# Pairing half-height matmuls as row tiles of TensorE in a matrix-LSTM followed by a rational feed-forward

## The chip, the cores and the metric

The kernel runs on one core of a Trainium2 chip (trn2). The metric is the device time of one execution in microseconds (us), of which the median of three runs is taken. A core has five engines that run side by side, each in the order of its own instruction stream: TensorE (PE, with its weight loads as PEld), VectorE (DVE), ScalarE (ACT), GpSimd (POOL) and SyncE (SP), which here issues nearly all DMAs. TensorE writes to PSUM, eight banks of 128 partitions by 512 f32 values.

## The reference

A matrix LSTM runs over 768 time steps for 4 batches and 8 heads of width 40, and its output, as 3072 tokens of 320 features, goes through a feed-forward layer whose activation is a rational function. Inputs are drawn at random; the feed-forward weights arrive as 64-bit floats.

```python
for t in range(S):
    m_new = np.maximum(f_gate[:, :, t] + m, i_gate[:, :, t])
    f_stab = np.exp(f_gate[:, :, t] + m - m_new)
    i_stab = np.exp(i_gate[:, :, t] - m_new)
    C = f_stab[..., None, None] * C + i_stab[..., None, None] * np.einsum('bhd,bhe->bhde', vt, kt)
    n = f_stab[..., None] * n + i_stab[..., None] * kt
    h_tilde = np.einsum('bhde,bhe->bhd', C, qt)
    denom = np.maximum(np.abs(np.einsum('bhd,bhd->bh', n, qt)[..., None]), 1.0)
    y[:, :, t] = sigmoid(o_gate[:, :, t]) * h_tilde / denom
...
h = x @ w_in                        # 320 -> 2048
P = a[0] + a[1] * h + a[2] * h**2 + a[3] * h**3
Q = 1.0 + np.abs(b[0]) * np.abs(h) + np.abs(b[1]) * h**2
out = (P / (Q + 1e-06)) @ w_out     # 2048 -> 320
```

## The kernel before

Time is cut into chunks of 64. One **unit** (`attention(u)`, 24 of them) is one batch over 128 time steps, that is two chunks, for all 8 heads. In a unit TensorE transposes keys and queries (`kq`), multiplies them to scores (`f_S`, tiles `ps0`, `ps1`: 16 matmuls of 40 rows by 64 columns that sit on the four 64x64 quadrants of the array), and VectorE multiplies the scores by the decay (`f_P`). Then `f_ow` sums each chunk's contribution to the state, for each head one matmul with all 128 rows and 64 columns of the array and 82 moving columns, whose value tile `vb` is half zeros, into a bank of its own, `ow`. VectorE adds that to the decayed state (`update`, in the list `u0` and `u1`), GpSimd decays the state (`d0`, `d1`). Two units make a **pair** (`outputs(m)`, 12 of them): `f_it` (16 matmuls of 128x64) and `inter` (32 or 16 on quadrants) write the read-out `y`, ScalarE takes the absolute normalizers (`f_ab`) into an SBUF tile `na`, VectorE inverts them (`f_rc`), and the result is transposed into tokens (`f_xt`, tile `px`) and split into a rounded part and a rest (`f_xh`, `f_xl`) in the tile `xk`.

A pair's 256 tokens are one **block** of the feed-forward. `feed_forward(n, i)` is step i (0 to 7) of block n: it handles two chunks of 128 hidden features. The 320 input features are three slices of 128, 128 and 64, each as rounded part and rest, so that a chunk takes eight matmuls of 256 columns into the bank `h` (in the trace `ph`): six with `wi`, one with `wj`, which has the 64-row slice of rounded weights twice, against rounded tokens above and their rest below, and one with `wY`, which has the rest of the 64-row slice of the weights in its upper 64 rows and zeros below:

```python
parts = [
    (w[:, 0, 0], 0), (w[:, 1, 0], 0), (w[:, 0, 1], 1), (w[:, 1, 1], 1),
    (w[:, 0, 0], 2), (w[:, 0, 1], 3), (wX, 4), (wY[:, c * P : (c + 1) * P], 4),
]
```

The activation then goes over ScalarE (`ha`, `p1`, `u`, `y`, `r0`), VectorE (`p3`, `gh`, `m`, `gl`) and GpSimd (`w`, `rm`), and `f_f2` multiplies the result, again as rounded part `gH` and rest `gL`, by `wo` into two banks `po`: per step 16 matmuls of 320 columns with `gH`, 8 with `gL`. All other PSUM tiles share six banks, the ring `h`; a tile takes a bank at its first write and gives it back with its last read.

Each step of work is an entry of a plan (`plan.add` with what it reads and writes). The text `ORDER` lists all entries in the order in which they are issued, so it fixes the stream of every engine; `_Ordered` keeps it. An entry is named by its step: `f1_5_2` is the first matmul of block 5, step 2, and `.1` marks the second of that name. At the start TensorE also runs 90 dummy matmuls (`hot`), and the weights are brought from 64 bits to rounded part and rest by ScalarE, VectorE and GpSimd.

Of the kernel before, what the change touches and what calls it, by code (L numbers as in the profile page):

```python
# [12 lines left out]
I32 = mybir.dt.int32  # L13
# [144 lines left out]
hot.63 hot.64 hot.65 hot.66 gate.11 raw_j0 o2_o0 ogl_0 o2_o3 qa_1 o0_i1 hot.67 P_1 P_1.1 s1_i3 gate.3 s0_i6 s1_i6
s3_i6 ow_1 o2_i1 s0_j1 s2_j1 s3_i3 o0_i3 hot.68 hot.69 hot.70 hot.71 hot.72 o2_i3 lk_2 s1_j1 hot.73 s3_j1 u0_1 o0_i6
o2_i6 s0_i2 gate.18 ogl_2 d1_1 pf_2 it_0 it_0.1 i1_0 sc_2 gate.12 o0_j1 o2_j1 lq_2 hot.74 lk_3 hot.75 s2_j0 s2_i2  # L160
s0_j0 ab_0 hot.76 s1_i2 s3_i2 hot.77 kp_2 o2_j1.1 ke_2 s1_j0 ogl_1 s3_j0 ogl_3 tk_2 ek_2 squares gate.19 ab_0.1 raw_o7
hot.78 hot.79 hot.80 hot.81 o0_j0 lq_3 gate.21 gate.13 hot.82 u1_1 gate.14 raw_i7 tq_2 eq_2 pf_3 kp_3 S_2 P_2 P_2.1
o2_j0 oc_j0 raw_o2 og_0 tk_3 ek_3 o2_j0.1 s0_o7.1 sc_3 gate.15 rc_0 s2_o7 hot.83 g_0 x_0 g_0.1 hot.84 hot.85 hot.86
lf_4 o0_i2 tq_3 s0_o7 s1_o7.1 ke_3 hot.87 hot.88 s3_o7.1 eq_3 x_0.1 xt_0 hot.89 gate.16 lv_2 s1_o7 s3_o7 gate.1 xh_0
xh_0.1 o0_o7 lk_4 s0_i7 S_3 oc_j1 xl_0 s2_i7 xl_0.1 f1_0_0 f1_0_0.1 gate.17 lv_3 P_3 s1_i7 qa_2 s0_o2.1 s1_o2.1 s0_o2
s2_o2 qa_3 raw_i5 o2_o7 o2_i2 f1_0_1 s3_o2.1 ow_2 ha_0_0 u_0_0 gate.20 lk_5 f1_0_1.1 s1_o2 P_3.1 u0_2 f1_0_2 s3_o2
w_0_0 d1_2 p1_0_0 p3_0_0 s3_i7 y_0_0 kp_4 o0_o2 o2_o2 sc_4 r0_0_0 u1_2 ow_3 gh_0_0 ha_0_1 u0_3 la_4 u_0_1 p1_0_1 lq_4
d1_3 m_0_0 f1_0_2.1 ha_0_2 p1_0_2 u1_3 p3_0_1 it_1 it_1.1 i1_1 w_0_1 rm_0_0 p3_0_2 ab_1 ab_1.1 rc_1 gl_0_0 u_0_2 y_0_1
tk_4 g_1 x_1 s0_i5 s2_i5 s1_i5 s3_i5 ke_4 w_0_2 f2_0_0 f2_0_0.1 f3_0_0 g_1.1 la_5 r0_0_1 y_0_2 r0_0_2 ek_4 kp_5 lq_5
f1_0_3 f1_0_3.1 f1_0_4 f3_0_0.1 ha_0_3 u_0_3 tq_4 eq_4 gh_0_1 m_0_1 f2_0_1 x_1.1 gh_0_2 p1_0_3 m_0_2 d0_4 o0_i7  # L170
f1_0_4.1 ha_0_4 rm_0_1 gl_0_1 o0_i5 p3_0_3 w_0_3 y_0_3 raw_o6 S_4 f2_0_1.1 f3_0_1 P_4 f3_0_1.1 f2_0_2 tk_5 f2_0_2.1
rm_0_2 gl_0_2 P_4.1 p1_0_4 r0_0_3 gh_0_3 ek_5 p3_0_4 o2_i5 m_0_3 f1_0_5 f3_0_2 f3_0_2.1 tq_5 f2_0_3 f1_0_5.1 f2_0_3.1
f1_0_6 u_0_4 qa_4 w_0_4 raw_o4 s0_o4.1 s1_o4.1 lf_5 lf_6 s2_o4 s3_o4.1 rm_0_3 eq_5 s0_o6.1 s0_o4 s2_o6 sc_5 lk_6 s1_o4
s1_o6.1 s3_o4 gl_0_3 y_0_4 r0_0_4 f1_0_6.1 gh_0_4 lv_4 o0_o4 ha_0_5 f3_0_3 ke_5 ogl_10 lv_5 lq_6 s3_o6.1 S_5 p1_0_5
ogl_6 f3_0_3.1 m_0_4 P_5 o2_i7 f1_0_7 f1_0_7.1 s0_o6 ha_0_6 u_0_5 o2_o4 s1_o6 P_5.1 rm_0_4 f2_0_4 s3_o6 u_0_6 p1_0_6
xt_1 gl_0_4 f2_0_4.1 ow_4 f3_0_4 p3_0_5 f3_0_4.1 xh_1 xh_1.1 xl_1 xl_1.1 o0_o6 u0_4 kp_6 tk_6 p3_0_6 w_0_5 y_0_5
r0_0_5 w_0_6 y_0_6 d1_4 u1_4 gh_0_5 m_0_5 la_6 f1_1_0 f1_1_0.1 r0_0_6 ek_6 qa_5 gh_0_6 d0_5 ow_5 gate.24 rm_0_5 u0_5
m_0_6 f2_0_5 ha_0_7 ha_1_0 u_0_7 p1_0_7 f1_1_1 f1_1_1.1 f2_0_5.1 gl_0_5 d1_5 gate.22 u1_5 u_1_0 p3_0_7 f3_0_5 f3_0_5.1
gate.23 lk_7 lf_7 lq_7 ogl_7 ogl_8 w_0_7 y_0_7 it_2 it_2.1 i1_2 ogl_11 rm_0_6 gl_0_6 tq_6 r0_0_7 gh_0_7 m_0_7 o2_o6
f2_0_6 f2_0_6.1 ha_1_1 p1_1_0 p1_1_1 p3_1_0 lv_6 sc_6 w_1_0 lv_7 p3_1_1 eq_6 rm_0_7 f3_0_6 f3_0_6.1 u_1_1 ab_2 y_1_0  # L180
w_1_1 r0_1_0 ab_2.1 gh_1_0 gl_0_7 f1_1_2 f1_1_2.1 ha_1_2 y_1_1 r0_1_1 rc_2 g_2 f2_0_7 f2_0_7.1 m_1_0 x_2 f3_0_7
# [190 lines left out]
def _program(  # L372
# [327 lines left out]
    def setup():  # L700
# [729 lines left out]
```

## Time and profile before

| | us |
|---|---|
| median of 3 runs | 514.77 (514.66 to 520.2) |
| profiled execution | 514.69 |
| its span, first to last instruction | 512.9 |
| TensorE busy in the span | 483.8 |
| VectorE, GpSimd, ScalarE busy | 426.0, 404.9, 402.4 |

The span is what the trace covers; some 1.8 us of the execution lie around it. Nearly every instruction is recorded under line 34, the helper that keeps the order, so instructions are told apart by the tile that they write and the tiles that they read (`ph<-xk,wY`) and by their shape. A shape such as 128*64 128x82 is rows times columns of the array that are in use, then the operand. A matmul on plain f32 tiles (`ps`, `ow`, `y`) shows as two records, one on fp32r tiles (`ph`, `po`) as one. The time of one matmul in the trace runs until its result has left the array, so it is longer than the distance at which matmuls follow one another; what a matmul costs is read from the distance between starts.

### The profile page before, as it was taken

What the parts mean: (1) busy time and instruction counts of PE and PEld (TensorE: products, weight loads), DVE (VectorE), ACT (ScalarE), POOL (GpSimd) and SP (SyncE); (2) the same over time, 40 slices, a digit from 0 to 9 for tenths busy, and PEclk for the clock granted to TensorE, in tenths of its full rate; (3) what the DMA queues carried; (4) which work ended last, traced back from release to release, by engine and by line L of the source; (5) the groups of instructions that cost most, each with busy time, mean ns of one, the idle gap of its engine ahead of it and who ended that gap; (6) DMA issues with size and microseconds to landing.
All of it is one profiled execution on the core that took longest, in us unless ns stands there. A gap on an engine that the chain in (4) does not pass through costs nothing.

```text
span 512.9 us, 14161 instructions
## 1 busy us (share of the span) xinstructions
PE 483.8 (94%) x5631; PEld 465.4 (91%) x5631; DVE 426.0 (83%) x702; ACT 402.4 (78%) x698; POOL 404.9 (79%) x375
## 2 busy tenths in 40 slices
PE   6898779999999999999999999999999999999991
PEld 6797679989999999999999999999999999999990
DVE  7889789889898988898797987877878787787890
ACT  1887788978798787788887789898778788869960
POOL 3679778989899988878787898868777889776770
PEclk9899899999999999999999999999999999999996
DMA  6998897415244341532422335311240120000001
GB/s 169 213 273 161 192 255 123 72 27 123 54 99 104 92 77 25 138 77 70 81 54 58 83 75 102 89 25 49 45 96 19 34 72 0 8 23 1 27 0 33
DMA packets 119117, 42.53 MB, mean 83 GB/s; under 512 B 103554, under 2 KB 111810, under 8 KB 119042
## 3 DMA queue, kind: packets, MB, share of 16 engines
q1 hardware_dynamic: 118912, 41.37, 37.0%
q8 instruction: 46, 0.75, 0.6%
q14 instruction: 29, 0.24, 0.2%
q10 hardware_dynamic: 130, 0.16, 0.1%
HBM read 36.90 MB, written 4.10 MB: 80 GB/s over the span
## 4 chain that ended last, share of the span: by engine, by line
PE 71%; DVE 9%; ACT 5%; DMA 4%; POOL 4%; issue 3%; SPq 1%; POOLq 0%; DVEq 0%; ACTq 0%
PE ph L34 29%; PE po L34 27%; PE y L34 4%; PE kq L34 3%; PE ow L34 3%; PE ps L34 2%; DMA rawo<-in_moe_w_out_dram 2%; DVE p L34 2%; POOL p L34 2%; DVE w L34 1%; PE px L34 1%; DMA rawi<-in_moe_w_in_dram 1%; DVE gL L34 1%; ACT ph L34 1%; DVE gH L34 1%
## 5 line engine op out<-in xcount | busy, mean ns | idle before, releaser
L34 POOL TENSOR_TENSOR p<-p,w 128x512 f32<-128x512 f32 (+1 forms) x97 | 129.5, 1335 | 56.4 <-DVE w L34 55.1
L34 PE MATMUL ph<-xk,wi 128*128 128x256 f32 x1152 | 167.5, 281 | 0.7 <-DVE pm L34 0.4
L34 PEld LDWEIGHTS ph<-xk,wi 128*128 128x128 f32 x1152 | 150.3, 188 | 1.8 <-ACT lo0i L34 0.6
L34 POOL TENSOR_TENSOR w<-w,ha 128x512 f32<-128x512 f32 (+1 forms) x97 | 129.9, 1343 | 10.7 <-ACT w L34 10.2
L34 PE MATMUL po<-wo,gH 128*128 128x320 f32 x768 | 135.5, 312 | 0.1
L34 PEld LDWEIGHTS po<-wo,gH 128*128 128x128 f32 x768 | 115.4, 188 | 1.3 <-DVE gH L34 0.3
L34 DVE SCALAR_TENSOR_TENSOR w<-w,gH 128x512 f32<-128x512 f32 (+1 forms) x97 | 89.5, 922 | 3.9
L34 ACT ACTIVATE ph<-w,cd 128x512 f32<-128x512 f32 (+1 forms) x97 | 66.5, 686 | 28.8 <-POOL w L34 14.4
L34 DVE SCALAR_TENSOR_TENSOR gL<-p,ps,ph 128x512 fp32r<-128x512 f32 (+1 forms) x97 | 71.0, 733 | 21.0 <-POOL p L34 20.0
L34 DVE SCALAR_TENSOR_TENSOR gH<-p,ps,ph 128x512 fp32r<-128x512 f32 (+1 forms) x97 | 71.2, 734 | 15.9 <-ACT ph L34 14.6
L34 PE MATMUL po<-wo,gL 128*128 128x320 f32 x384 | 79.8, 318 | 4.3 <-DVE gL L34 4.2
L34 ACT ACTIVATE w<-ha,ba 128x512 f32<-128x512 f32 (+1 forms) x97 | 78.4, 811 | 3.0
L34 DVE SCALAR_TENSOR_TENSOR p<-p,ps,ph 128x512 f32<-128x512 f32 (+1 forms) x97 | 70.6, 733 | 10.8 <-ACT p L34 10.6
L34 ACT ACTIVATE ha<-ph 128x512 f32<-128x512 f32 (+1 forms) x97 | 57.2, 592 | 24.4 <-PE ph L34 23.6
L34 ACT ACTIVATE p<-ph,ps 128x512 f32<-128x512 f32 (+1 forms) x97 | 65.5, 676 | 2.1 <-DVE gL L34 1.8
L34 PEld LDWEIGHTS po<-wo,gL 128*128 128x128 f32 x384 | 59.0, 188 | 7.5 <-DVE gL L34 6.5
L34 ACT ACTIVATE ph<-ph 128x512 f32<-128x512 f32 (+1 forms) x97 | 56.1, 579 | 2.1
L34 PE MATMUL ph<-xk,wY 128*128 128x256 f32 x192 | 53.5, 279 | 0.0
L34 PE MATMUL ph<-xk,wj 128*128 128x256 f32 x192 | 53.4, 278 | 0.0
L34 PEld LDWEIGHTS ph<-xk,wj 128*128 128x128 f32 x192 | 36.2, 188 | 0.0
L34 PEld LDWEIGHTS ph<-xk,wY 128*128 128x128 f32 x192 | 36.1, 188 | 0.0
L34 POOL TENSOR_TENSOR qA<-qT,ab 104x512 f32<-104x512 f32 x24 | 32.0, 1334 | 0.0
(128 smaller groups left out, 658.7 us busy)
## 6 DMA issues: line engine op xcount, KB each, us to landing
rawo<-in_moe_w_out_dram SPq DMA_DIRECT2D x8, 640.0 KB
ab<-scrA SPq DMA_DIRECT2D x40, 128.0 KB
rawi<-in_moe_w_in_dram SPq DMA_DIRECT2D x8, 512.0 KB
qn<-in_q_dram SPq DMA_DIRECT2D x24, 160.0 KB
kr<-in_k_dram SPq DMA_DIRECT2D x24, 160.0 KB
og<-in_o_gate_dram SPq DMA_DIRECT2D x48, 80.0 KB
vb<-in_v_dram SPq DMA_DIRECT2D x48, 80.0 KB
out_dram<-ot SPq DMA_DIRECT2D x23, 160.0 KB
```

The source lines that it names most:

```text
L34: made = fn(*args, **kwargs)
```

## The change

- **Half matmuls.** `wY` is now half as wide and carries the rest of two steps' weights, one in its upper 64 rows, one in its lower. A new entry `f0` for each two steps i and i+1 opens the banks of both and issues four matmuls of 64 rows by 128 columns, alternating between the upper rows (step i) and the lower rows (step i+1); `f1` is left with seven matmuls a chunk. The tokens' rounded 64-row slice is needed in the lower rows too, so ScalarE copies it a second time (`xh` has three entries a pair, `xk` six slices).
- **Step order.** The two steps of an `f0` must use the two halves of `wY`, so step i handles chunks 2*PI[i] and 2*PI[i]+1, with PI = 0, 4, 1, 5, 2, 6, 3, 7.
- **State sums.** `f_ow` issues 16 matmuls of 64 rows, 64 columns and 41 moving columns on quadrants, chunk 0 into the rear of score bank `ps0`, chunk 1 of `ps1`. The bank `ow` is gone; `ps0` is given back after `u0`, `ps1` after `u1`.
- **Normalizers.** `f_ab` writes both halves to the rear of the bank of `y0`, and `f_rc` reads them there.
- **Weights.** The rest of the 64-row slice is loaded in four pieces instead of two; the clearing of `wY`'s lower half by GpSimd goes.
- **List.** `ORDER` is a new list over the new entries.

```diff
-    wY = wp.tile([P, DFF], F32R, name="wY")
+    wY = wp.tile([P, DFF // 2], F32R, name="wY")
...
-            subtract(wY[0:L, c : c + n], z[rr[j]], t[rr[j], cols[j]])
+            subtract(wY[rr[j], s * n : (s + 1) * n], z[rr[j]], t[rr[j], cols[j]])
...
-            ow = d["ow"] = bank("ow")
-            for h in range(H):
-                p, j = divmod(h, 2)
-                nc.tensor.matmul(
-                    ow[j * L : (j + 1) * L, p * 2 * E1 : (p + 1) * 2 * E1],
-                    d["pm"][:, h, 0:L],
-                    vs[:, h].rearrange("p c e -> p (c e)"),
...
+            d["ow"] = [d["ps"][c][:, NP * L :] for c in range(2)]
+            for p in range(NP):
+                for j in range(2):
+                    for c in range(2):
+                        r = slice(c * L, (c + 1) * L)
+                        nc.tensor.matmul(
+                            d["ow"][c][j * L : (j + 1) * L, p * E1 : (p + 1) * E1],
+                            d["pm"][r, 2 * p + j, 0:L],
+                            vs[r, 2 * p + j, c],
...
-        add("ow", "PE", 0.85, f_ow, r=["pm.1", "pm.00", "pm.01", V], w=["ow"], new=new("ow"))
+        add("ow", "PE", 0.85, f_ow, r=["pm.1", "pm.00", "pm.01", V], w=["ps0", "ps1"])
...
-            nc.scalar.copy(xk[nb][:, 0:2, tk] if x == 0 else xk[nb][0:L, 4, tk], pm(x))
+            nc.scalar.copy((xk[nb][:, 0:2, tk], xk[nb][0:L, 4, tk], xk[nb][L:P, 5, tk])[x], pm(min(x, 1)))
...
+    PI = [c // 2 + c % 2 * NS // 2 for c in range(NS)]
...
+        def f_f0():
+            at = iter(plan.many["h"])
+            for x in range(2):
...
+                    FD[n, i + x]["h", j] = ring(psH, "h", [P, W], f"ph{n}_{i + x}_{j}", at=next(at))
+            for j in range(2):
+                for x in range(2):
+                    t, r = FD[n, i + x], slice(x * L, (x + 1) * L)
...
+                    nc.tensor.matmul(
+                        to[:, 0:T], wY[r, c : c + P], xk[n][r, 4 + x, 0:T], start=own, stop=False, skip_group_check=True
+                    )
...
-                (w[:, 0, 0], 2), (w[:, 0, 1], 3), (wX, 4), (wY[:, c * P : (c + 1) * P], 4),
+                (w[:, 0, 0], 2), (w[:, 0, 1], 3), (wX, 4),
```

**TensorE around the start of a block, before.** `px` are the transposes of new tokens, `ph` the hidden features of step 0 of a block.

```order
L34 MATMUL px_6_4022<-ident,xn_3818 128x128 x4
L34 MATMUL px_6_4023<-ident,xn_3818 64x128 x2
L34 MATMUL ph_0_0_4030<-xk_3546,wi_442 128x256 x6
L34 MATMUL ph_0_0_4030<-xk_3546,wj_776 128x256
L34 MATMUL ph_0_0_4030<-xk_3546,wY 128x256
L34 MATMUL ph_0_0_4030<-xk_3546,wi_442 128x256 x6
L34 MATMUL ph_0_0_4030<-xk_3546,wj_776 128x256
L34 MATMUL ph_0_0_4030<-xk_3546,wY 128x256
L34 MATMUL po_0_3608<-wo_451,gL_5_4000 128x320
```

**The same place after.** The first row is the last of a unit's scores, `ph_0` and `ph_1` are the banks of steps 0 and 1 of the block.

```order
L34 MATMUL ps_12_3497<-qT_127,kT_3262 64x64
L34 MATMUL ph_0_0_3514<-xk_2914,wY 128x256
L34 MATMUL ph_1_0_3515<-xk_2914,wY 128x256
L34 MATMUL ph_0_0_3514<-xk_2914,wY 128x256
L34 MATMUL ph_1_0_3515<-xk_2914,wY 128x256
L34 MATMUL ph_0_0_3514<-xk_2914,wi_359 128x256 x6
L34 MATMUL ph_0_0_3514<-xk_2914,wj_723 128x256
L34 MATMUL ph_0_0_3514<-xk_2914,wi_359 128x256 x6
L34 MATMUL ph_0_0_3514<-xk_2914,wj_723 128x256
L34 MATMUL ph_1_0_3515<-xk_2914,wi_444 128x256 x6
L34 MATMUL ph_1_0_3515<-xk_2914,wj_723 128x256
```

The two `wY` matmuls of each step have left the chunks and stand together ahead of two steps' chunks, and both steps' banks are written from there on; here they follow the scores directly.

**TensorE around a unit's state sums, before.** The two `ow` are two units, between the second product of one step and the first product of another.

```order
L34 MATMUL po_0_3608<-wo_905,gL_7_4172 128x320
L34 MATMUL po_1_3609<-wo_905,gL_7_4172 128x320
L34 MATMUL ow_4179<-vb_62,pm_3857 64x82 x8
L34 MATMUL ow_4205<-vb_129,pm_4099 64x82 x8
L34 MATMUL ph_3_0_4214<-xk_3546,wi_646 128x256 x6
L34 MATMUL ph_3_0_4214<-xk_3546,wj_725 128x256
```

**State sums after.** These rows are the last two of one unit's 16 (`ps_12_...<-vb,pm`), then the next `f0` and the second product of an earlier step.

```order
L34 MATMUL ps_12_3496<-vb_62,pm_3493 64x41
L34 MATMUL ps_12_3497<-vb_62,pm_3493 64x41
L34 MATMUL ph_2_0_3636<-xk_2914,wY 128x256
L34 MATMUL ph_3_0_3637<-xk_2914,wY 128x256
L34 MATMUL ph_2_0_3636<-xk_2914,wY 128x256
L34 MATMUL ph_3_0_3637<-xk_2914,wY 128x256
L34 MATMUL po_0_3108<-wo_1209,gH_7_3561 128x320 x2
L34 MATMUL po_1_3109<-wo_1209,gH_7_3561 128x320 x2
```

A unit's state sums are now 16 matmuls of 41 columns that alternate between the two score banks; in this place an `f0` follows them. Over the whole program the shape of the tile that TensorE works with (128x128, 128x64, 64x64, 64x128; transposes count as 128x128) changes 119 times in the stream before and 207 times in the stream after. Of the 48 `f0`, in 46 stretches, 27 stretches come after 128x128 work and 19 after 64x64 work; 43 are followed by 128x128 work and 3 by 64x64 work.

## Rows read from the trace of the kernel before

**Rows 1.** The page: engines' busy time, and the chain by engine

```profile
PE 483.8 (94%) x5631; PEld 465.4 (91%) x5631; DVE 426.0 (83%) x702; ACT 402.4 (78%) x698; POOL 404.9 (79%) x375
...
PE 71%; DVE 9%; ACT 5%; DMA 4%; POOL 4%; issue 3%; SPq 1%; POOLq 0%; DVEq 0%; ACTq 0%
```

**Rows 2.** Busy time by stretch, us; (x) is instructions; then PEclk, DMA share, GB/s

```profile
0.00:60.00 60.00, 48.95 (x713) 45.34 (x714) 49.18 (x121) 40.18 (x73) 40.51 (x51) 0.94 0.89 208
60.00:110.00 50.00, 45.80 (x563) 42.00 (x562) 44.26 (x75) 42.69 (x77) 43.50 (x40) 1.00 0.68 130
...
200.00:300.00 100.00, 99.95 (x1210) 96.86 (x1206) 85.64 (x131) 81.97 (x140) 82.85 (x76) 1.00 0.37 79
```

**Rows 3.** TensorE's waits: us in total, times, longest us

```profile
PE po L34 <- DVE gL L34: 4.2, 8, 1.1
```

**Rows 4.** Groups by shape: busy us, mean ns of one, idle us before

```profile
L34 PE MATMUL ph<-xk,wY 128*128 128x256 f32 x192 | 53.5, 279 | 0.0
...
L34 PEld LDWEIGHTS ph<-xk,wY 128*128 128x128 f32 x192 | 36.1, 188 | 0.0
...
L34 PEld LDWEIGHTS ow<-vb,pm 128*64 128x64 f32 x384 | 14.9, 136 | 3.7 <-issue 1.5 <-DVE zo L34 0.6 <-DVE gL L34 0.2
...
L34 PEld LDWEIGHTS ps<-qT,kT 40*64 40x64 f32 x768 | 13.6, 135 | 4.1 <-issue 1.1 <-ACT qT L34 0.9 <-ACT wo L34 0.2
...
L34 ACT CAST xk<-px 64x256 fp32r<-64x256 f32 x12 | 4.4, 367 | 0.0
```

**Rows 5.** Timeline of PE, us 256 to 258: start, time to last end

```profile
256.21 0.87 PE L34 MATMUL ph<-xk,wi 128*128 128x256 f32 x6
256.92 0.28 PE L34 MATMUL ph<-xk,wj 128*128 128x256 f32 x1
257.04 0.28 PE L34 MATMUL ph<-xk,wY 128*128 128x256 f32 x1
257.15 0.75 PE L34 MATMUL po<-wo,gL 128*128 128x320 f32 x4
```

**Rows 6.** Timeline of PE, us 286 to 290: the scores between whole-array work

```profile
286.30 0.28 PE L34 MATMUL ph<-xk,wY 128*128 128x256 f32 x1
286.50 0.69 PE L34 MATMUL ps<-qT,kT 40*64 40x64 f32 x32
287.13 0.85 PE L34 MATMUL po<-wo,gL 128*128 128x320 f32 x4
287.81 1.33 PE L34 MATMUL po<-wo,gH 128*128 128x320 f32 x8
288.99 0.75 PE L34 MATMUL po<-wo,gL 128*128 128x320 f32 x4
```

**Rows 7.** Timeline of PE, us 273 to 277: reading out a pair

```profile
273.62 0.28 PE L34 MATMUL ph<-xk,wY 128*128 128x256 f32 x1
273.82 1.35 PE L34 MATMUL y<-vb,pm 128*64 128x82 f32 x32
275.11 0.68 PE L34 MATMUL y<-st,qA 40*64 40x41 f32 x32
275.59 0.66 PE L34 MATMUL y<-sm,qA 40*64 40x41 f32 x32
276.18 0.86 PE L34 MATMUL po<-wo,gH 128*128 128x320 f32 x4
276.88 0.75 PE L34 MATMUL po<-wo,gL 128*128 128x320 f32 x4
```

**Rows 8.** Timeline of PE, us 265 to 268: state sums of two steps

```profile
265.18 0.74 PE L34 MATMUL po<-wo,gL 128*128 128x320 f32 x4
265.86 1.35 PE L34 MATMUL ow<-vb,pm 128*64 128x82 f32 x32
267.14 0.96 PE L34 MATMUL ph<-xk,wi 128*128 128x256 f32 x6
267.94 0.28 PE L34 MATMUL ph<-xk,wj 128*128 128x256 f32 x1
```

More of the change, by code (lines that the diff above doesn't have):

```diff
@@ L804, in loads @@
             for j in range(2):
-                c = (2 * j + s) * n
-                yield raw[rr[j]].rearrange("p f w -> p (f w)"), w_in[2 * P : DM, c : c + n].bitcast(I32)
+                for h in range(2):
+                    c = (2 * j + s) * n + h * n // 2
+                    to = raw[rr[j], h * n // 2 : (h + 1) * n // 2].rearrange("p f w -> p (f w)")
+                    yield to, w_in[2 * P : DM, c : c + n // 2].bitcast(I32)
         def high(t, z):
@@ L983, in update @@
         def update(c, dst):
[L985 removed]
+            own = d["ow"][c][0:DP, 0 : NP * E1].rearrange("p (n e) -> p n e", n=NP)
             if n + c == 0:
@@ L1040, in attention @@
             outputs(u // 2)
-        add("u1", "DVE", 0.66, lambda: update(1, st[now]), r=["t1"], w=["ow", *ST3])
+        add("u1", "DVE", 0.66, lambda: update(1, st[now]), r=["t1"], w=["ps1", *ST3])
     def outputs(m):
@@ L1077, in f_ab @@
         def f_ab(k):
[L1078 to L1080 removed]
+            to = d[0][:, NA + k * H : NA + (k + 1) * H].rearrange("p (h c) -> p h c", h=4)
+            nc.scalar.activation(to, ye(k)[:, :, :, D], AF.Abs)
         def f_rc():
[L1083 removed]
+            d["na"] = ring(ap1, "na", [P, 2, H], f"na{m}")
+            nc.vector.tensor_scalar(
+                d["na"], d[0][:, NA : NA + 2 * H].rearrange("p (k h) -> p k h", k=2), 1.0, None, op0=ALU.max
+            )
             nc.vector.reciprocal(d["na"], d["na"])
@@ L1150, in outputs @@
         first = [(X, ("xk", XB))] if m == firsts_of[nb] else ()
-        for x in range(2):
-            add("xh", "ACT", 0.42, lambda x=x: f_xh(x), r=[px[x]], w=[f"{X}.{m - firsts_of[nb]}{x}"], new=first if x == 0 else ())
+        for x in range(3):
+            add("xh", "ACT", 0.42, lambda x=x: f_xh(x), r=[px[min(x, 1)]], w=[f"{X}.{m - firsts_of[nb]}{x}"], new=first if x == 0 else ())
         for x in range(2):
@@ L1338, in each @@
                 )
-        xs = [f"xk{n}.{j}{x}" for j in range(size) for x in range(2)]
+        xs = [f"xk{n}.{j}{x}" for j in range(size) for x in range(3)]
+        if i % 2 == 0:
+            hs = [f"h{n}_{i}"]
+            hs += [f"h{n}_{i + 1}p{j}" for j in range(2)] if n == len(SIZES) - 1 and i + 1 >= NS - HALVED else [f"h{n}_{i + 1}"]
+            ws = [f"wj{PI[i] // 2}{x}" for x in ("", ".l")]
+            plan.add(
+                f"f0_{n}_{i}", "PE", 0.25, f_f0, [xs[1], xs[2], *ws], [*hs, "turn f0"], [(h, ("h", BANKS)) for h in hs]
+            )
         for j in range(2):
             f = chunk(j)
-            add("f1", "PE", 0.9, lambda j=j: f_f1(j), w=["h"], new=[("h", ("h", BANKS))] if j == 0 or last else (), part=j,
-                r=[*xs, f"wi{f // 2}", f"wi{f // 2}.l",
-                   *(f"wj{f % 8 // 4}{x}" for x in ("", ".x", ".l"))])
+            add("f1", "PE", 0.82, lambda j=j: f_f1(j), w=["h"], part=j,
+                r=[*xs, f"wi{f // 2}", f"wi{f // 2}.l", *(f"wj{f % 8 // 4}{x}" for x in ("", ".x"))])
         each("ha", "ACT", 0.48, f_ha, w=["h", "ha"], tag="ha")
```

369 lines of the change are left out of this document (184 added, 185 removed).

## The prediction

> **What bounds the kernel now.** I read the page's busy times first: TensorE is busy for 94% of the span, VectorE for 83%, the others for less, and the chain that ended last runs over TensorE for 71% [rows 1]. An average hides stages, so the table by stretch comes second. Up to 110 us TensorE is busy for 48.95 + 45.80 = 94.75 us, part of that with dummy matmuls; from 200 to 300 us it is busy for 99.95 of 100, at a granted clock of 1.00, which is the 2.4 GHz level, while VectorE, ScalarE and GpSimd stand at 82 to 86 [rows 2]. Third, the waits of TensorE: the largest entry is 4.2 us in 8 waits for the last vector operation of a step [rows 3]. So from about 110 us on the time is the length of TensorE's own stream, and whatever the change does to the other engines is hidden as long as they stay under it. "Busy" means occupied, not working at its peak. What the stream is made of shows only in the timeline, fourth, by the distance between starts.
>
> **Prices from the timeline.** Six matmuls of 256 columns take 256.92 - 256.21 = 0.71 us, so one takes 0.118, and the `wY` one takes as long (0.11 to the next start) although half of its rows are zeros [rows 5]. Eight `po` matmuls take 1.18 us, 0.148 each [rows 6]. On quadrants 32 records take 275.59 - 275.11 = 0.48 us, 0.015 each [rows 7].
>
> Next to these there is a price that no busy time shows: a change of tile shape. From the start of `wY` at 286.30 to the second `po` group at 287.81 are 1.51 us [rows 6]. One `wY` (0.12), 32 records on quadrants (0.48) and four `po` (0.59) explain 1.19. The other 0.32 are two changes, from 128x128 to 64x64 and back, 0.16 each. One sees it directly too: `ps` starts 0.20 after `wY`, where 0.11 is usual. The two units' sums from 265.18 to 267.94 are 2.76 us; without four `po` (0.59), six `wi` (0.71) and two changes (0.32), 1.14 stay for 32 records of `ow`, 0.57 a unit [rows 8]. The read-out confirms it with three changes: 3.26 us, less 0.12, 0.59, 32 records of 128x64 work (1.14) and 64 on quadrants (0.96), leaves 0.45, which is 0.15 for each, and one of these, from 128x64 to 64x64, changes the rows of the tile alone [rows 7]. I take 0.155.
>
> **The change part by part.** The sums are made on TensorE's stream of the profiled execution, 514.69 us, of which 512.9 are span; the median of the runs is 514.77, so nothing has to be scaled.
>
> Half matmuls, gain: 192 `wY` slots of 0.118, 22.6 us, go [rows 4, 5]. In their place are 48 `f0` of two slots each, if the upper and the lower tile run side by side. Quadrant work shows that tiles overlap (0.015 a record against 0.036 for 128x64) [rows 7, 8]. With 0.12 a slot that is 11.5 us, a gain of 11.1. If they do not overlap, the gain is nothing; these are the two ends, and I take the first, as the nearest row (quadrants) overlaps.
>
> Half matmuls, price: 64x128 is a shape of its own. The stream changes shape 207 times instead of 119. I see no row for a change from 128x128 to 64x128; the nearest is the one that changes rows alone, and it is charged [rows 7]. 88 more changes at 0.155 are 13.6 us. A change also lays the first weight load bare, and a load of 128 columns is recorded with 188 ns, one of 64 columns with 136 and 135, whether it has 128 or 40 rows [rows 4]; 46 entries into 64x128 therefore cost another 0.05 each, 2.4 us. Together 16.0. A lone `f0` between 128x128 work is thus 0.24 + 0.31 + 0.05 = 0.60 us against the 0.47 that it replaces; one beside 64x64 work adds one change only, 0.45, and breaks even. The other end: if a change between 128x128 and 64x128 is free, 137 changes are left that are charged, 18 more than before, 2.8 us.
>
> The Trainium skill, TensorEngine Tiling (Array Packing), Key Properties, says that a change of the tiling mode, and not of the tile, drains the engine. This trace agrees for every pair of shapes in it (0.15 to 0.16 us each); for 64x128 no run here shows it, and by that rule the sum stays as it is. The Trainium skill, TensorE: Matmul & The Clock Gate, Part 3 (Packing small matmuls), counts a group of tiles as one matmul plus some 4 ns a tile, with no charge for coming and going. By that rule `f0` only gains, which is the first rival below; the rows for 64x64 speak against it.
>
> State sums: 32 records on quadrants take 0.48 us where 16 of 128x64 took 0.57 [rows 7, 8]; 24 units gain 2.2 us. Their changes of shape are in the count above. Ends: 0 and, if 41 columns ran faster than the read-out's 41 do, hardly more.
>
> Sum over the stream: -11.1 - 2.2 + 16.0 = +2.7 us. About a ninth of the `f0` and a quarter of the units lie ahead of 110 us, where TensorE has slack; nine tenths of it, +2.4, count.
>
> Banks: `f0` needs the banks of both steps at once, a step earlier than before for the second, and `ps0` and `ps1` stay taken until the state is updated, while the bank `ow` is gone. If a bank comes late, the four `f0` matmuls wait, and behind them all that TensorE has in its stream (both steps' chunks, the products of earlier steps, the scores), and then ScalarE waits for `ph`. The nearest row for such a wait is 4.2 / 8 = 0.5 us [rows 3]. I charge two or three of them, 1 us; the low end is nothing.
>
> Nothing for the rest: the third `xh` is 12 copies of 0.367 us, 4.4 us on ScalarE [rows 4], which has 18 of 100 us to spare [rows 2]; if it were late, one `f0` in four would feel it, 12 times 0.37. The normalizers are as many instructions as before. The cleared half of `wY` saves GpSimd work at the start. Four more DMAs are issued by SP at the start, for the same bytes. The new list: at the first steps the other engines have about the same work ahead of them in both streams, so I give it no sign, and 3 us either way, of the 15 that TensorE is not busy ahead of 110 us [rows 2].
>
> Forecast: 514.7 + 2.4 + 1 = **518 us**, no change that a measurement of this kernel can tell, since that takes about 2%, 10 us.
>
> **Rivals.** (1) Coming to and from 64x128 is free. Then -11.1 - 2.2 + 2.8 = -10.5, nine tenths of it -9.4, and with 1 us of waits 506. For it: no row shows this very change. Against it: the change of rows alone in the read-out is charged [rows 7].
> (2) Slower: the two tiles of an `f0` take turns instead of overlapping. Place: each `f0`; price: 96 more slots of 0.118, 11.3 us, nine tenths of them 10, so 528. It decides from where two thirds of the overlap are lost, as 525 is 7 us above the forecast. For it: no row shows tiles with 128 columns side by side. Against: 64x64 tiles in different rows overlap.
> (3) Slower: banks. If half of some 43 `f0` in the bound part wait 0.5 us, 11 us more than the forecast has without waits: 528. For it: two banks of six at once, and score banks that stay taken. Against: one bank less a unit, and a TensorE stream that is longer leaves the others more time.
> (4) Faster: the new list fills the start better and (1) holds in part: half of the price that (1) drops (6 us) and 5 of the 15 us ahead of 110 give 507, all of it and the 5 give 501.
>
> **How the numbers follow.** Forecast 0.60, (1) 0.17, (2) 0.08, (3) 0.08, (4) 0.07. The forecast's own range is 513 to 524, from the list's 3 us and the waits. The 8-in-10 range reaches to (1) below and (2) and (3) above: 505 to 529. Faster by over 2% (under 504.5): a third of (1) and most of (4), 0.11. Slower by over 2% (over 525): most of (2) and (3) and a little of the forecast, 0.17. Within 2%: 0.72.
>
> **What would show it.** In the timeline after: `wY` starts in pairs within some 10 ns, two pairs 0.12 apart (otherwise (2)); the first `wY` starts about 0.20 after a 256-column matmul and the second `wi` after an `f0` about 0.22 after the first (if 0.12 both times, (1)). TensorE should be busy for over 99 of 100 us from 200 to 300; if it is not and `ph` waits for the last vector operation of a step stand in the list of waits, (3). The forecast is wrong if a lone `f0` takes under 0.45 us from its place, or if the start of the steady stretch moves by more than 5 us.

## The result, and the profile after

The changed kernel takes 521.9 us (median of 16 runs, 517.72 to 523.02); the kernel before takes 514.86 us beside it. By the medians it is slower by 7.0 us. The ratio, which is that of the means of the runs, is 1.0118 (6.1 us), with a 95% interval from 1.0097 to 1.0139: a little over 1%, less than the 2% that the forecast set as its line, and 3.9 us above the 518 forecast. The profiled execution took 520.92 us with a span of 519.1, and is the one read here, against 514.69 and 512.9 of before.

The page of the kernel after: busy times by engine, and the chain that ended last, by engine. They answer to [rows 1].

```profile
PE 487.8 (94%) x6015; PEld 458.8 (88%) x6015; DVE 420.3 (81%) x702; ACT 407.7 (79%) x710; POOL 398.3 (77%) x374
...
PE 81%; DVE 5%; SPq 4%; DMA 3%; ACT 2%; issue 2%; DVEq 0%; ACTq 0%
```

TensorE is the bound even more than before, 81% of the chain against 71, and its busy time rose by 4 us. Weight loads take 459 us for 465, though 384 more of them are recorded, those of the state sums. ScalarE has the twelve added copies. (A step has 8 products of 320 columns with `gH` and 4 with `gL`, 768 and 384 in all, and not the 16 and 8 that the description of the kernel gives; the sums of the prediction do not use these counts.) On the engines nothing looks seven microseconds worse, so the next view is the one by stretch, with the columns of [rows 2].

```profile
0.00:60.00 60.00, 49.45 (x813) 45.04 (x813) 46.98 (x117) 37.88 (x68) 35.57 (x49) 0.94 0.89 205
60.00:110.00 50.00, 43.86 (x538) 40.44 (x537) 43.71 (x76) 44.31 (x82) 42.53 (x38) 0.93 0.61 129
110.00:200.00 90.00, 87.74 (x1081) 82.13 (x1080) 78.12 (x120) 71.56 (x124) 75.86 (x70) 0.98 0.34 71
200.00:300.00 100.00, 100.00 (x1275) 94.77 (x1274) 81.76 (x129) 81.82 (x141) 80.22 (x73) 1.00 0.35 74
```

The reader should see two things. From 200 us on TensorE is busy for 100 of 100 us, as forecast. And from 60 to 200 us something is new in the column of the granted clock: 0.93 and 0.98, where before stands at 1.00 from 60 to 110 [rows 2], and from 110 to 200 too. From 60 to 110 TensorE also does less, 43.86 us of busy time against 45.80. Its waits there, in the view of waits from 60 to 120 us (us in total, times, longest us):

```profile
PE po L34 <- DVE gL L34: 2.3, 1, 2.3
PE ph L34 <- DVE zi L34: 2.1, 1, 2.1
PE po L34 <- DVE gH L34: 2.0, 1, 2.0
PE kq L34 <- issue: 1.9, 1, 1.9
```

Four waits of about 2 us each, 8.3 us in all. Before has nine waits in the same stretch, 5.4 us in all, and none is longer than 1.1; the largest entry there is

```profile
PE po L34 <- DVE gL L34: 3.1, 4, 1.1
```

The price of the pairs is read from the timeline of the kernel after (start, time to the last end, operation):

```profile
227.96 0.83 PE L34 MATMUL po<-wo,gL 128*128 128x320 f32 x4
228.71 0.68 PE L34 MATMUL ps<-vb,pm 64*64 64x41 f32 x32
229.32 0.50 PE L34 MATMUL ph<-xk,wY 64*128 64x256 f32 x4
229.75 1.44 PE L34 MATMUL po<-wo,gH 128*128 128x320 f32 x8
231.03 0.75 PE L34 MATMUL po<-wo,gL 128*128 128x320 f32 x4
...
237.66 1.34 PE L34 MATMUL po<-wo,gH 128*128 128x320 f32 x8
238.84 0.45 PE L34 MATMUL po<-wo,gL 128*128 128x320 f32 x2
239.23 0.50 PE L34 MATMUL ph<-xk,wY 64*128 64x256 f32 x4
239.66 0.97 PE L34 MATMUL ph<-xk,wi 128*128 128x256 f32 x6
240.46 0.28 PE L34 MATMUL ph<-xk,wj 128*128 128x256 f32 x1
...
275.67 0.74 PE L34 MATMUL ph<-xk,wY 64*128 64x256 f32 x8
276.34 0.97 PE L34 MATMUL ph<-xk,wi 128*128 128x256 f32 x6
```

A lone `f0` first: from 237.66 to 240.46 are 2.80 us; ten `po` at 0.148 and six `wi` at 0.118 explain 2.19, so four half matmuls with their way in and out cost 0.61 us, where the four whole ones cost 0.47. That the tiles overlap is seen at 275.67: two `f0` in one stretch last 0.67 us to the next start, one lasts 0.43 at 239.23, so four more records take 0.24, which is 0.12 for a pair of an upper and a lower tile. The single starts in the trace say the same: in the long stretch the pairs start at 275.67, 275.89, 276.01 and 276.13, the two tiles of a pair 3 or 4 ns apart. The 0.22 between the first two pairs is the price of coming in; in a lone `f0` it stands between its only two pairs (239.23 and 239.45). Beside 64x64 work, from 227.96 to 231.03, 3.07 us less twelve `po` (1.77) and 32 quadrant records (0.48) leave 0.81; 0.32 of it the quadrants would have cost alone [rows 6], so this `f0` adds 0.49 and about breaks even.

So the tiles of a pair run side by side, and the way in and out costs about what was forecast. What remains to be found is where the seven microseconds come from.

### The profile page after: what moved, and what is told of

The parts are those of the page before. It is cut to its first block, busy times and chain, and to the rows that moved or that the text cites. A ratio compares the mean times of both kernels' runs of the same rounds, so it can differ in the third digit from the quotient of the medians.

```text
span 519.1 us, 14993 instructions
## 1 busy us (share of the span) xinstructions
PE 487.8 (94%) x6015; PEld 458.8 (88%) x6015; DVE 420.3 (81%) x702; ACT 407.7 (79%) x710; POOL 398.3 (77%) x374
## 4 chain that ended last, share of the span: by engine, by line
PE 81%; DVE 5%; SPq 4%; DMA 3%; ACT 2%; issue 2%; DVEq 0%; ACTq 0%
PE ph L34 34%; PE po L34 32%; PE ps L34 5%; SPq L34 4%; PE y L34 4%; PE kq L34 4%; DMA vb<-in_v_dram 2%; PE px L34 1%; DMA rawo<-in_moe_w_out_dram 1%; ACT ph L34 1%; DVE gH L34 1%; DVE gate_f L34 1%; DVE e L34 1%; DVE gL L34 0%; PE hot L34 0%
## 5 line engine op out<-in xcount | busy, mean ns | idle before, releaser
L34 POOL TENSOR_TENSOR p<-p,w 128x512 f32<-128x512 f32 (+1 forms) x97 | 127.1, 1310 | 60.2 <-DVE w L34 58.4
L34 POOL TENSOR_TENSOR w<-w,ha 128x512 f32<-128x512 f32 (+1 forms) x97 | 126.4, 1307 | 10.9 <-ACT w L34 10.6
L34 DVE SCALAR_TENSOR_TENSOR w<-w,gH 128x512 f32<-128x512 f32 (+1 forms) x97 | 79.9, 824 | 5.6
L34 PEld LDWEIGHTS po<-wo,gL 128*128 128x128 f32 x384 | 60.1, 191 | 5.0 <-DVE gL L34 3.6
L34 POOL TENSOR_TENSOR qA<-qT,ab 104x512 f32<-104x512 f32 x24 | 33.6, 1401 | 3.0 <-ACT qT L34 3.0
L34 PE MATMUL hot<-ident 128*128 128x128 f32 x180 | 27.2, 306 | 4.0 <-DVE flag_out L371 4.0
L34 PEld LDWEIGHTS hot<-ident 128*128 128x128 f32 x180 | 24.8, 217 | 4.5 <-issue 4.0
```

The lines of the kernel that those rows point to most:

```text
L34: made = fn(*args, **kwargs)
```

## Experiments

**The change taken apart.** The change has three parts: the list, the state sums on quadrants, and the pairs. Three theories stood against each other, and the expectations name them so: A, that of the prediction, by which the shape changes of the pairs cost somewhat more than the overlap gains, and the list is neutral; B, the pairs gain about 10 us and the list loses more than that; C, the pairs come out even and the list costs it all. The first experiment keeps the list and the quadrants of after and takes the pairing out, with the same number of instructions:

```
-  to[:, 0:T], wY[r, c : c + P], xk[n][r, 4 + x, 0:T], start=own, ...
+  to[:, 0:T], wY[:, c : c + P], xk[n][:, 4, 0:T], start=own, ...
```

> The changed kernel and its list, but the four matmuls of each f0 use all 128 rows (128x128, the paired weights against the token slice of step i), so no tile shape changes for them and nothing overlaps; the sums they add are not the reference's. The stream has 137 changes of shape instead of 207. Theory A (leaving and entering 64x128 costs more than the overlap gives): 70 changes at 0.155 us and 46 long loads at 0.05 go, 11.1 us of overlap go too; net 2 us faster, up to 4 if a lone f0 is 0.63 us against 0.47: 518 to 520. Rival B (pairing pays its 11 us and the loss is made by the list): 10 us slower, 531. Rival C (pairing is worth nothing either way): 522.

Measured: 518.11 us, ratio 1.0055 (1.0037 to 1.0073). The pairs cost 521.9 - 518.1 = 3.8 us in this list, as A has it; B and C don't fit.

The second takes the quadrants out as well, so that of the change the list stays, with what belongs to it: `f0` as an entry of its own ahead of two steps, now at full height, the step order, the third copy, the loads in four pieces, and the sums in a score bank. This is meant by the list alone below.

```
-  d["ow"] = [d["ps"][c][:, NP * L :] for c in range(2)]   # 16 matmuls of 64x64
+  ow = d["ow"] = d["ps"][1]                               # 8 matmuls of 128x64, as before
```

> The changed kernel's list with the old forms of both matmuls: f0 on all 128 rows as in e1, state sums as 8 matmuls of 128x64 with 82 columns, in the second score bank; the hidden features are not the reference's. 129 changes of shape. TensorE's work is then that of before plus ten changes (1.6 us). Theory A with a list that is no better or worse: 516. Rival (the list costs 3 to 5 us at the start, by more waits and a low clock): 518 to 521. Rival B: 525 or more is not expected by any.

Measured: 520.11 us, ratio 1.0092 (1.0061 to 1.0122). The list alone costs 5.2 us against 514.87 beside it; ten of its shape changes (129 for 119) are 1.6 of that by the prediction's price. From here to the first experiment are the quadrants, which gain 2.0 us. So 5.2 - 2.0 + 3.8 = 7.0 us, where each term is a difference of medians and uncertain by one to two us: the largest part is the one that I gave no sign. The quadrants were also taken out with the pairs kept, by the same edit:

> After with its list and its pairs, but the state sums as before: 8 matmuls of 128x64 tiles in the second score bank in place of 16 on quadrants. 24 units times 0.09 us more per unit is +2.2, 8 shape changes fewer at 0.155 are -1.2: +1 us by my terms, 522.5 to 523.5. Rival: the quadrants gain nothing, 521.5 to 522; or more than the row says, 524 to 525.

Measured: 522.43 us, ratio 1.0123 (1.0079 to 1.0167), 0.5 us above after. The interval holds the expected 1 us and the rival's nothing too; the times of this run do not decide it (its trace, below, does better).

**The parts in the old list.** The other way round, each part was put into the kernel before with its list; entries of the list for which a bank was not free yet were put later, up to where it is.

```
+  f0_n_i ahead of f1_n_i for each even i, opening the banks of steps i and i + 1
```

> The kernel before and its list, with the half matmuls paired alone: f0 stands right ahead of the first f1 of each even step, the third xh behind the second, natural step order (the two halves of the weights are loaded by even and odd steps). 218 changes of shape instead of 119; 45 of 48 f0 come after 128x128 work. Theory A: 99 changes at 0.155 are 15.3, 48 long loads 2.4, overlap 11.1 gained, net 6.6, nine tenths of it 6 us slower than before: 521. Rival B: 10 us faster than before, 505. Rival C: 515.

Measured: 571.44 us, ratio 1.1117 (1.1065 to 1.1168). All three theories missed by 50 us. TensorE's waits in this run (us in total, times, longest us):

```profile
PE y L34 <- DVE gL L34: 6.0, 4, 2.1
PE ph L34 <- DVE gL L34: 4.7, 4, 2.9
PE kq L34 <- ACT wi L34: 4.5, 1, 4.5
```

In the first two rows `y` and `ph` wait for `gl`, which makes none of their operands but is the last reader of a step's bank `h`: they wait for a bank. The third row names work on the weights, and what `kq` waits for there is not shown. With the state sums:

```
-  ow = d["ow"] = bank("ow")
+  d["ow"] = [d["ps"][c][:, NP * L :] for c in range(2)]
```

> The kernel before and its list, with the state sums alone changed: on quadrants in the rear of the score banks, no bank ow. 134 changes of shape instead of 119 (sums no longer share a shape with the read-out that follows some of them), 2.3 us; 24 shorter sums gain 2.2. Theory A: 515, as before. Rival (the bank that is given up, or banks that stay taken, decide): 4 us or more away from it.

Measured: 614.75 us, ratio 1.1924 (1.1894 to 1.1955), and the same picture in the first and the third row:

```profile
PE ph L34 <- DVE gL L34: 12.6, 8, 3.7
PE ph L34 <- DVE zo L34: 9.1, 2, 5.1
PE kq L34 <- DVE gL L34: 7.2, 5, 3.0
```

What follows: the parts put into the old list cost 57 and 100 us, and waits for banks, the prediction's third rival, are among the causes. They are not all of it: TensorE's waits sum to 49 and 81 us in these two traces and to 17.5 in before, its busy time rose too, from 483.8 to 508.8 and 520.1 us, with mean granted clocks of 0.968 and 0.929 for 0.985, and how much comes from entries that were put later was not separated. With the new list these waits are gone. The two runs say nothing of the parts' own price.

**The price of a shape change by itself.** In the kernel before, list and banks untouched, one matmul a step loses its 64 rows of zeros:

```
...
-  nc.tensor.matmul(to, w, x[:, kx], start=(o == 0), stop=(o == 7))
+  r = slice(0, L if o == 7 and j == 1 else P)
+  nc.tensor.matmul(to, w[r], x[r, kx], start=(o == 0), stop=(o == 7))
```

> The kernel before with its own list and banks; of each step's second half the matmul on the rest of the weights runs on rows 0 to 63 alone (a 64x128 tile, the other 64 rows were zeros). 96 matmuls of the same 256 columns, and 292 shape changes in place of 119. My theory (a change into or out of a row tile drains the array and shows the weight load): 173 changes at 0.155 us, or 77 whole stretches at the 0.39 us that the trace of after shows, are +27 to +30 us, 540 to 546 us. Rival 1 of the prediction (such changes are free): 514 to 516.

Measured: 543.53 us, ratio 1.0558 (1.0450 to 1.0667), 28.1 us above the 515.42 beside it. By 173 more changes that is 0.162 us for each (0.13 to 0.20 by the interval), and the prediction's first rival (a change to or from 64x128 is free) is out. The 0.162 has the longer weight load of 64x128 in it, and it spreads the price over changes ahead of 110 us too. By the prediction's own terms these runs would pay 173 x 0.155 + 96 x 0.05 = 31.6 us, nine tenths of it 28.5. The timeline of this run shows one:

```profile
265.39 0.87 PE L34 MATMUL ph<-xk,wi 128*128 128x256 f32 x6
266.10 0.28 PE L34 MATMUL ph<-xk,wj 128*128 128x256 f32 x1
266.31 0.38 PE L34 MATMUL ph<-xk,wY 64*128 64x256 f32 x1
266.62 0.85 PE L34 MATMUL po<-wo,gL 128*128 128x320 f32 x4
267.31 1.33 PE L34 MATMUL po<-wo,gH 128*128 128x320 f32 x8
```

`wY` starts 0.21 after `wj` where 0.11 is usual, `po` 0.31 after `wY`, and the next group only 0.69 after that instead of 0.59. From `wj` to the `gH` group are 1.21 us; two matmuls of 256 columns and four of 320 explain 0.83, the rest, 0.38, is the way in and out. The work is half the rows, and takes the same columns: fewer rows alone save nothing.

**Is TensorE the bound all the way?** After without the four half matmuls, their banks still opened at the same place:

```
-  nc.tensor.matmul(to[:, 0:T], wY[r, c : c + P], xk[n][r, 4 + x, 0:T], start=own, ...)
...
-  nc.tensor.matmul(to, w, xk[n][:, kx, 0:T], start=False, ...)
+  nc.tensor.matmul(to, w, xk[n][:, kx, 0:T], start=(o == 0 and (j == 0 or last)), ...)
```

> After with the four half matmuls of each pair of steps left out (the rest-of-weights term is not in the sum); their banks are still opened at the same place in the list. If TensorE sets the end all the way, as my sum took it, 48 times 0.24 us of bodies and 70 shape changes at 0.155 to 0.166 us go: -22 to -23, 498.5 to 500 us. Rival: other engines or the banks set part of the steady stretch in the new list, so that a shorter TensorE only waits: less than 15 us go, 507 or more.

Measured: 508.82 us, ratio 0.9851 (0.9769 to 0.9934): 13.1 us went, not 22, so the rival holds. TensorE's waits in this run from 110 to 490 us:

```profile
PE po L34 <- DVE gL L34: 5.4, 9, 2.3
PE y L34 <- DVE gL L34: 0.4, 1, 0.4
PE ps L34 <- DVE xn L34: 0.3, 1, 0.3
```

Nearly all of these 6.1 us are for a step's last vector operation. One of them, 2.3 us at 115, after has as well (2.3 us at 114); the other 3.8 us are new, since after has no wait at all from 125 to 500 us. So a TensorE stream that is some 4% shorter already meets the end of the activation. VectorE itself is not full there (83.07 of 100 us from 200 to 300): its `gL` in turn waits for GpSimd's `p`, 14.6 us in 21 waits from 125 to 490. The sum does not close: seven of the 48 `f0` lie ahead of 125 us, where TensorE waits anyway, and the other 41 at 0.47 us are 19.3, less 3.8 of new waits 15.5, where 13.1 went; the 2.4 us between them are not explained.

**Why the list costs.** The waits at the start came with a lower granted clock, in this list more than in the old one. By stretch, the kernel before and then the kernel after:

```profile
44.00:57.00 13.00, 8.51 (x111) 7.72 (x110) 10.28 (x26) 8.82 (x18) 11.19 (x12) 0.88 1.02 245
...
74.00:81.00 7.00, 6.75 (x78) 6.25 (x78) 6.83 (x9) 6.41 (x12) 6.37 (x8) 1.00 1.00 211
...
110.00:119.00 9.00, 7.91 (x89) 7.45 (x89) 8.32 (x14) 6.73 (x14) 7.62 (x7) 1.00 0.21 45
```

```profile
44.00:57.00 13.00, 9.48 (x129) 8.26 (x127) 9.84 (x25) 8.29 (x14) 7.02 (x9) 0.74 0.97 195
...
74.00:81.00 7.00, 5.10 (x22) 5.04 (x22) 6.27 (x13) 7.00 (x14) 7.00 (x7) 0.52 0.66 154
...
110.00:119.00 9.00, 6.74 (x39) 5.99 (x38) 8.89 (x13) 3.85 (x8) 5.79 (x7) 0.81 0.16 27
```

Each lower stretch comes with waits: at 114.27 us the products of a step had waited 2.26 us for `gL`, and the `wi` matmuls from 115.85 on take 0.24 us each instead of 0.12, the 1.2 GHz level. To test whether this is the price, matmuls of `ident` by `ident`, which nobody reads, were put ahead of six of the waiting instructions:

```
+  fill(HT["t"][:, 0:P], 6)                    # in f_tk of unit 3, f_ow of unit 2
+  fill(FD[n, i]["h", 0][:, 0:P], 9)           # in f_f0 of step 2
+  fill(PO[n][0][:, DM : DM + P], ...)         # 9, 8 and 10 ahead of f2_0_0, tq_4 and f3_0_7
```

> The changed kernel with its own list; in six places of the start where the trace of after shows PE waiting (before the sums of unit 2, the transposes of unit 3, the half matmuls of step 2, the first second-layer matmul, the query transposes of unit 4 and the low half of step 7) 6 to 10 matmuls of ident by ident are put ahead of the waiting one, into the bank of the warm-up matmuls or into columns that nothing reads; 48 in all, 0.2 us each, 10 us of work in about 12 us of waits. Theory W: what the list costs is the granted clock, 0.5 for 17.1 us of the start against 6.8 in before; with the waits filled the level stays up and 2 to 4 us come back: 518 to 520 us, mean clock 0.982 or more. Rival L: the waits themselves (data that come late by the list) are the price and the clock in them costs nothing: 521 to 523, and 1 to 3 more where the added matmuls push what follows.

Measured: 518.31 us, ratio 1.0048 (1.0009 to 1.0087), with a clock of 0.993 (in this run the added matmuls also begin new sums in the banks of block 0's output, so that block's sums are incomplete). The same stretches:

```profile
44.00:57.00 13.00, 12.24 (x200) 10.88 (x198) 10.17 (x29) 9.09 (x15) 10.13 (x12) 1.00 0.96 205
...
74.00:81.00 7.00, 6.94 (x55) 6.71 (x54) 6.28 (x13) 7.00 (x14) 7.00 (x7) 1.00 0.65 152
...
110.00:119.00 9.00, 9.00 (x74) 8.55 (x73) 8.92 (x12) 5.46 (x11) 5.80 (x6) 1.00 0.21 37
```

The clock stays at its upper level, and 3.6 us come back with 10 us of useless work added; the two intervals do not overlap. The same fills in the full-height kernel, in the list alone (there without the side effect on block 0), and in the kernel before at its own four waits:

> The kernel with the half matmuls on all 128 rows (sums of these four matmuls differ) and the six fills. Theory W: the pairing's price, 3.8 us between after and the full-height kernel, was partly the clock of the start, since the two profiles have 17.1 and 10.2 us at 0.5; between the filled pair it is 1.5 to 3 us. Rival A: it is the 70 shape changes, and stays 3.5 to 4.5 us below e8.

> The new list alone (half matmuls on all rows, sums as before in the second score bank, 129 shape changes) with the six fills of the start. Theory W: the list's 5.2 us are 1.6 of ten more shape changes and some 3 to 4 of the half clock in its start; filled it is 517 to 518 us with a mean clock of 0.988 or more, within 3 us of before. Rival L: the order itself (waits, work of the steady stretch) is the price and it stays at 519.5 to 521.

> The kernel before, with the same kind of matmul (20 in all) ahead of the four waits that precede its two stretches at half clock (transposes and scores of unit 0, query transposes of unit 3 with its wait of 2.95 us). Theory W: up to 3.4 us come back, half of that as the estimate: 512.5 to 514 us. Rival L: nothing comes back, 514.5 to 516.

Measured: full height 516.68 us, ratio 1.0025 (0.9980 to 1.0070), 1.4 us less than without fills; the list alone 518.89, ratio 1.0075 (1.0049 to 1.0100), 1.2 us less; the kernel before 515.02, ratio 1.0005 (0.9954 to 1.0057), nothing, though its mean clock rose from 0.985 to 0.989. In the first two the gain is smaller than their intervals. Theory W holds for the changed kernel. For the pairs the filled kernels differ by 518.31 - 516.68 = 1.6 us, by W 1.5 to 3, but their intervals overlap, so the times alone do not tell this from the 3.8. For the list W explains only part: 518.89 is 3.6 us above the 515.27 beside it, 1.6 of them by ten shape changes, and 2 us stay open. And W falls for the kernel before, where the rows show what became of the gain. First before, then the same two places with the fills:

```profile
54.14 1.07 PE L34 MATMUL kq<-ident,qn 128*104 128x128 f32 x4 [2.95 <-DMA qn<-in_q_dram]
...
60.76 0.97 PE L34 MATMUL ph<-xk,wi 128*128 128x256 f32 x6 [0.36 <-DVE pm L34]
```

```profile
53.24 0.60 PE L34 MATMUL kq<-ident,qn 128*104 128x128 f32 x4
...
60.26 0.99 PE L34 MATMUL ph<-xk,wi 128*128 128x256 f32 x6 [2.19 <-DVE pm L34]
```

The filled transposes come 0.9 us earlier and run at the upper level, and the first `wi` matmuls 2.4 us earlier (55.89 for 58.30). But the next group must wait for VectorE's `pm`, now 2.19 us instead of 0.36, the granted clock is 0.50 from 61.2 to 64.4 us behind that wait, and the first product of the second layer starts at 70.82, where before had 70.72. Here the time that TensorE gained was lost in its next wait for another engine.

**Where along the execution the time is lost.** The traces tell the start from the steady stretch. Give every matmul the price of the prediction (0.118 for one of 256 columns and for a `wY` in either form, 0.148 for a `po`, 0.015 a record on quadrants, 0.57 for a unit's sums in either form, 0.57 for the 128x64 work of a unit in the read-out, 0.06 a record for transposes, nothing for dummies and fills) and add them up in order of time; then see how much later a run has issued the work that before has issued at 120 us. It is an estimate, from one execution of each kernel, and it moves by up to one us with the place of an entry in the list.

| | us behind before at 120 us | at the end |
|---|---|---|
| list alone | 2.6 | 3.7 |
| full height | 5.4 | 4.5 |
| the change | 5.7 | 6.2 |
| list alone, filled | 1.6 | 2.8 |
| full height, filled | 2.3 | 1.3 |
| the change, filled | 3.1 | 3.8 |

So of the 6.2 us in these profiles 5.7 are lost by 120 us (5.3 by 140), and the whole steady stretch adds under 1. The fills give back their 2.4 us in the start and nothing behind it. In the steady stretch, counted from 120 or from 140 us, the parts come out nearly alike with and without fills: the list costs 1.1 to 1.6 us, the quadrants gain 1.9 to 2.2 (1.6 to 1.8 between after and the run with the old sums), and the pairs cost 1.3 to 1.6. Of the 3.8 us of the pairs by the medians some 1.5 are thus paid in the bound part; the rest would lie in the start, where the runs differ most, and is not shown to be a price of the pairs.

**A version to beat both?** If a shape change costs 0.16 us, moving lone state sums beside other small tiles should help the kernel before:

```
-  ... ow_4 f3_0_4 ... ow_5 ... it_2        ow_8 ... S_9        ow_14 ... ow_15 ... it_7
+  ... ow_4 ow_5 it_2                       ow_8 S_9            ow_14 ow_15 it_7
```

> The kernel before with five entries of its list moved: the state sums of units 4, 5, 8, 14 and 15 from alone among 128x128 work to beside the read-out or the scores that follow; 112 shape changes in place of 119, the same work. By 0.16 us a change 1.1 us go where TensorE is the bound: 513.5 to 514.5 us, below both kernels. Rival: the state update that now comes later makes VectorE or a bank late: 515 to 517.

Measured: 523.94 us, ratio 1.0172 (1.0141 to 1.0204): 8.7 us slower, the rival, and by far more than it said. Seven changes went and waits came. Entries that need a moved one go behind it, the state updates on VectorE above all, so the order of VectorE and GpSimd changes too. From the timeline of this run (idle time before it and its releaser in brackets), and its busy times by stretch:

```profile
163.97 0.79 PE L34 MATMUL ow<-vb,pm 128*64 128x82 f32 x16
164.68 0.69 PE L34 MATMUL ps<-qT,kT 40*64 40x64 f32 x32
165.31 0.56 PE L34 MATMUL po<-wo,gL 128*128 128x320 f32 x2
167.39 0.93 PE L34 MATMUL ph<-xk,wi 128*128 128x256 f32 x6 [1.52 <-DVE st L34]
```

```profile
200.00:300.00 100.00, 97.08 (x1150) 93.92 (x1149) 80.79 (x125) 78.76 (x134) 77.66 (x73) 0.98 0.34 70
```

The moved sum (`ow` at 163.97) is read by the state update `st`, which now ends late, and the step behind it waits 1.52 us for the bank. By the count of issued work the loss comes in steps at the moved places, 1.6 us around 168 us and 4.9 between 260 and 280, and 3.4 are there already at 120. No version that makes all the sums of the reference beat the kernel before.

## Why the prediction was right, and where it was short

**Right: the bound.** TensorE busy for over 99 of 100 us from 200 to 300: it is 100.00. But its lead is small: some 22 us less TensorE work gave 13. The forecast for a faster outcome, rivals (1) and (4), would have been capped by this; the prediction did not price it.

**Right: the pairs.** The gain of 11.1 us by overlap: four more records in one stretch take 0.24 us, so a pair takes one slot, and rival (2) is out. One of the prediction's own signs was set wrongly: two pairs 0.12 apart were to tell against (2), but in a lone `f0` they start 0.22 apart, because the price of coming in stands between them; only in the longer stretch are the later pairs 0.12 apart. The price: 0.155 a change was taken from 64x64 work and carried to 64x128; one run with 173 more changes gave 0.162, with the longer load in it. The Trainium skill, TensorEngine Tiling (Array Packing), Key Properties, says that a change of the tiling mode drains the engine; this run agrees, with that number beside it. The Trainium skill, TensorE: Matmul & The Clock Gate, Part 3 (Packing small matmuls), gives a packed group the time of one matmul and some 4 ns a tile. That holds for the tiles themselves (two start 3 or 4 ns apart, 0.12 us a pair); the way in and out (0.38) comes on top, and here it decides. A lone `f0` was put at 0.60 us and takes 0.61; beside 64x64 work it was put at 0.45 and takes 0.49. By the prediction's terms the pairing's seventy changes are 10.9 us and the longer load 2.4, against 11.1 gained: +2.2, nine tenths of it 1.9. From 120 us on the traces show some +1.5.

One reading under the 0.155 is weaker than it looks: 0.57 for a unit's sums took its two changes from [rows 6], and the 0.15 from 128x64 to 64x64 rests on that 0.57. Solved together without it, [rows 7] and [rows 8] give 0.13 a change and 0.60 a unit. With 0.13 throughout the forecast would have been two to three us lower, farther from the result.

**Right in sign: the state sums.** -2.2 for the work, of which 8 more changes take back 1.2, so -1.0; measured -2.0 between two runs and -2.2 between their filled kin, while the third comparison, 522.43 against 521.9, cannot tell it from nothing. In the traces all three show a gain of 1.6 to 2.2 us in the steady stretch, about twice what was forecast for the whole. With 0.60 a unit and 0.13 a change, as above, the terms would give -1.8; whether that is the reason was not tested.

**Not seen as a cost: the banks.** I charged 1 us. From 120 to 500 us the changed kernel has no wait of TensorE for a bank or for `gL`. In the old list the same parts cost 57 and 100 us. The mechanism of rival (3) is among what these runs show, and the new list is what answers it.

**The step that was short** is the one on the new list: "at the first steps the other engines have about the same work ahead of them in both streams, so I give it no sign, and 3 us either way". The list alone costs 5.2 us (3.1 to 6.3 by its interval). Part of it is work that my own count had (ten changes, 1.6 us). Another part is a thing that I had not asked of the rows at all: four waits of 2 us in place of nine shorter ones, and with them a granted clock of 0.93 from 60 to 110 us and 0.98 to 200. From [rows 2] and the same table of after, time lost to the clock is 50 x 0.07 + 90 x 0.02 = 5.3 us more than before, if TensorE were the bound throughout; it is not, and filling the waits brought 3.6 back. What is left of the list, some 2 us by the medians, lies in the start by the traces: filled, the list alone is 1.6 us behind at 120 us and loses 1.2 behind that, no more than its ten changes cost by the prediction's price. Which entries of the start make it was not settled.

That 521.9 lies so near 518 is in part luck. By the count above the start lost 5.7 us where the forecast had nothing, and the steady stretch lost under 1 where it had 2.4, with 1 more for banks that no row behind 120 us shows.

By the forecast's own tests: no lone `f0` was under 0.45. It also called itself wrong if the start of the steady stretch, which it put at about 110 us, moves by more than 5 us. By the work issued it moved by 5.1 us at 110 and by 5.0 to 5.7 from there to 150, so this sign stands at its limit, and the step it points at is the one just named. (The first product of the second layer starts only 1.9 us later, at 72.64 against 70.72, but two of the four long waits come behind it.) The outcome lies in the 513 to 524 of the likeliest case.

## What to carry to other kernels

Before packing two half-height matmuls side by side, count how often the stream will change its tile shape: here a change cost 0.16 us, a stretch between whole-array work 0.38, so four matmuls of 256 columns saved 0.24 and paid 0.38. Eight of them in one stretch, two `f0`, come out a little ahead: in the one at 275.67 they took 0.85 us with both changes, for 0.94 replaced. Longer stretches should gain more, which no run here tried. And where an order is derived anew, look at how its idle time is distributed, not only at its sum: behind a few waits of 2 us the granted clock was half, while the same list with the waits filled by useless matmuls was faster. It was faster only where no other engine held TensorE up next: in the kernel before the gain went into the next wait.

## What the runs showed of the hardware that I had not expected

Work that nobody needs made a kernel faster: 48 added matmuls, 10 us of them, 521.9 to 518.3 us, with the clock at 0.993 instead of 0.976. Among the 16 runs of the changed kernel the two with the highest mean clock, 0.986, took 517.72 and 520.05 us and the two with the lowest, 0.973, took 521.78 and 523.02.

A shape change costs about the same whichever pair of shapes it joins: 0.16 us for 128x128 to 64x64 [rows 6], 0.13 to 0.15 where 128x64 is one of the two [rows 7, 8] and, by 173 of them, 0.16 for 64x128 with its longer load.

Five entries of a list of 2719, moved by 11 to 59 places, with the entries that need them behind them, cost 8.7 us, more than the whole change.
